# Chunk attention and a feed-forward layer on one core: scores and values as four 64x64 tiles from the tenth group on

## The chip, the cores and the metric

The kernel runs on one core of one Trainium2 chip. The metric is the device time of an execution in microseconds (us). Three runs of the kernel before took 304.3, 305.3 and 305.69 us; their median is 305.3 us.

## The reference

The inputs q, k and v are 8 batches x 8 heads x 576 positions x 64 in float32. Attention stays within chunks of 64 positions, so a batch has nine chunks:

```
scores = scale * q_c @ k_c^T            # 64 x 64 for each batch, head and chunk
scores = scores - max(scores)
attn   = exp(scores);  attn = attn / (sum(attn) + 1e-9)
out    = attn @ v_c                     # 64 x 64
x = out laid out as (8*576 tokens, 8*64 = 512)
h = x @ w_in                            # 512 -> 2048
y = maximum(0.01 h, h) @ w_out          # 2048 -> 512
```

The output is 4608 x 512 in float32.

## The kernel before, in words

The 4608 tokens go through attention in 36 groups (u = 0 to 35) of two chunks (128 tokens, all eight heads). The result of a group is written transposed into xT (features on partitions, tokens along the free axis), and the feed-forward layer takes xT in blocks of 128, 256 and 512 tokens (BLOCKS, L57). All is computed in float16 with float32 sums.

A group passes through these stages, each a function:

- The transposes of q and k. Groups 0 to 8 load token rows (load_qk, L71) and transpose them on TensorE (stage_t, L255) into the PSUM tiles qp and kp; DVE copies q to QZ and ACT copies k to KT. From group UD = 9 on, that is from batch 2 on, load_qk_batch (L89) brings a whole batch in blocks of 32 to the tiles q_d and k_d, and DVE transposes the blocks straight into QZ (stage_dq, L290, one call for each half s of the partitions) and KT (stage_dk, L298).
- Scores (stage_s, L306). Two heads sit on the 128 partitions of q and k, each with its 64 features. QZ holds each q block in a 128x128 frame whose other two quarters are zeros, so that one matmul gives 64 scores of two heads on 128 output partitions. Eight matmuls of 64 columns fill the PSUM tile Sp.
- Softmax: stage_m (L316, DVE: maximum and subtraction from PSUM), stage_x (L325, ACT: exp), stage_n (L329, DVE: sum, reciprocal, product into en).
- The transposes of en (stage_e, L342, four on TensorE into tpe) and their copy by DVE (stage_c, L349) to et.
- Values (stage_v, L355). VB holds v of one batch with a zero block beside each 64 columns; there are two such buffers. Eight matmuls of 64 columns fill xp. stage_a (L372, ACT) copies xp to xT.

The feed-forward layer is cut into chunks of work: mm1 (L161: matmuls from w_inT and xT into hT, then ACT's leaky ReLU into gT) and mm2 (L182: four matmuls from gT and w_outT into oP, after the last of four ACT's copy to osb and the store). fill(n) (L228) issues the next n chunks whose tokens are there.

The order on each engine is the order of the program text, written by hand. The first five groups and the start of others follow the list FRONT (L415), with dummy matmuls ("i"). The loop at L428 does the rest: in turn it come scores and softmax of group it-1, a fill of 2 chunks, the transposes of en of group it-2, the q and k transposes of group it, again 2 chunks, the values of group it-2, then 3 chunks. So each turn has 28 matmuls of the feed-forward layer of 512 columns, once the blocks are large. What is left of that layer follows the loop.

All loads go through POOL's queue in program order: first the list LOADS (L147: g for q and k of a group, v for a batch of v, Q and P for quarters of the weights, D2 for q and k of batch 2), then v of batch b+2 after the last values of batch b (L368), and q and k of batches 3 to 7 at turns given by L454. The stores go through SP's queue.

PSUM has eight banks: mm takes four, qp, kp, Sp and ox (shared by tpe and xp) one each.

Of the kernel before, what the change touches and what calls it, by code (L numbers as in the profile page):

```python
# [8 lines left out]
FP16 = mybir.dt.float16  # L9
FP32 = mybir.dt.float32  # L10
ALU = mybir.AluOpType
AFT = mybir.ActivationFunctionType
AXL = mybir.AxisListType
# [3 lines left out]
def kernel(  # L17
# [6 lines left out]
    moe_w_out: bass.AP,  # L24
    out: bass.AP,
):

    nc = tc.nc

    B, H, S, D = q.shape
# [3 lines left out]
    CH = 64  # L45
    NCH = S // CH
# [3 lines left out]
    NQZ = 3  # L50
    NVB = 2
    NIN = 9
    UD = 9
    G = 2 * CH
# [4 lines left out]
    sbp = ctx.enter_context(tc.tile_pool(name="k_sb", bufs=1))  # L59
    psp = ctx.enter_context(tc.tile_pool(name="k_ps", bufs=1, space=bass.MemoryType.PSUM))  # L60
# [2 lines left out]

    VB = [sbp.tile([128, H // 2, NCH, 128], FP16, name=f"VB{i}") for i in range(NVB)]
    QZ = [sbp.tile([128, 4, 2, 2, CH], FP16, name=f"QZ{i}") for i in range(NQZ)]
    w_inT = sbp.tile([128, NT, d_ff], FP16, name="w_inT")
    w_outT = sbp.tile([128, NFC, d_model], FP16, name="w_outT")
    xT = sbp.tile([128, NT, n_tok], FP16, name="xT")
# [40 lines left out]
    def load_v(b):  # L109
        for m in range(2):  # L110
            nc.gpsimd.dma_start(  # L111
                out=VB[b % NVB][m * CH:(m + 1) * CH, :, :, m * CH:(m + 1) * CH].rearrange("p h c d -> p (h c) d"),
                in_=v[b, m * H // 2:(m + 1) * H // 2].rearrange("h (c j) d -> j (h c) d", j=CH),
            )

    def load_w_in(f0, f1):
        for m in range(2):
            nc.gpsimd.dma_start(  # L118
                out=w_inT[m * CH:(m + 1) * CH, :, f0:f1],
                in_=moe_w_in[m * d_model // 2:(m + 1) * d_model // 2, f0:f1].rearrange("(t d) f -> d t f", d=D),  # L120
            )
# [14 lines left out]
    for eng, name, src in ((nc.sync, "q_f", q), (nc.scalar, "k_f", k)):  # L136
        t = sbp.tile([128, H, D], FP32, name=name)
# [7 lines left out]
    qk[0] = tuple(sbp.tile([128, H, D], FP16, name=n, tag=n, bufs=NIN) for n in ("q_in", "k_in"))  # L145

    LOADS = (  # L147
        "g1 v0 Q1 Q0 g2 Q2 Q3 g3 g4 P0 g5 P2 P3 P1 g6 v1 g7 g8 D2 "
    )
    LOADERS = {"g": load_qk, "v": load_v, "Q": load_w_in_quarter, "P": load_w_out_quarter, "D": load_qk_batch}  # L150
    ident = sbp.tile([128, 128], FP16, name="ident")
    for n, what in enumerate(LOADS.split()):
        LOADERS[what[0]](int(what[1:]))
        if n == 0:
# [6 lines left out]
    def mm1(j, a):  # L161
        tb, r0 = BLOCKS[j], START[j]
        nf = 512 // tb
        if j not in gT:
            tag, bufs, pad = ("gS", 6, 128) if tb == 128 else ("gT", 2, 512)
            gT[j] = sbp.tile([128, NFC, tb], FP16, name="gT", tag=tag, bufs=bufs, padded_shape=[128, NFC, pad])
        hT = psp.tile([128, nf, tb], FP32, name="hT", tag="mm", bufs=4)
        for i in range(nf):
            fc = nf * a + i
            for t in range(NT):  # L170
                nc.tensor.matmul(  # L171
                    out=hT[:, i, :],
                    lhsT=w_inT[:, t, fc * 128:(fc + 1) * 128],
                    rhs=xT[:, t, r0:r0 + tb],
                    start=(t == 0),
                    stop=(t == NT - 1),
                )
        nc.scalar.activation(  # L178
            out=gT[j][:, nf * a:nf * a + nf, :], in_=hT, func=AFT.Prelu, bias=0.0, scale=1.0, alpha=0.01
        )  # L180
# [45 lines left out]
    state = {"tokens": 0}  # L226
# [19 lines left out]
    KP: dict[int, bass.AP] = {}  # L246
    SP: dict[int, bass.AP] = {}
    KT: dict[int, bass.AP] = {}
    SH: dict[int, bass.AP] = {}
    E: dict[int, bass.AP] = {}  # L250
    TP: dict[int, bass.AP] = {}
# [2 lines left out]

    def stage_t(u):  # L255
        qt, kt = qk.pop(u)
        qp = psp.tile([128, 4, 2, CH], FP16, name="qp", tag="qp", bufs=1)
        kp = psp.tile([128, 4, 2, CH], FP16, name="kp", tag="kp", bufs=1)
        for i in range(4):
            nc.tensor.transpose(out=qp[:, i, :, :], in_=qt[:, 2 * i:2 * i + 2, :], identity=ident)  # L260
        for i in range(4):
            nc.tensor.transpose(out=kp[:, i, :, :], in_=kt[:, 2 * i:2 * i + 2, :], identity=ident)  # L262
        QP[u], KP[u] = qp, kp

    def stage_q(u, halves=(0, 1)):
        for s in halves:
            part = slice(s * CH, (s + 1) * CH)
            nc.vector.tensor_copy(out=QZ[u % NQZ][part, :, :, s, :], in_=QP[u][part])

    def stage_w(u, halves=(0, 1)):  # L270
        for s in halves:
            part = slice(s * CH, (s + 1) * CH)
            nc.scalar.activation(
                out=QZ[u % NQZ][part, :, :, s, :], in_=QP[u][part], func=AFT.Copy, bias=0.0, scale=1.0
            )
# [9 lines left out]
    def cuts(u):  # L285
        r0, r1 = u * G, (u + 1) * G
        cut = min(-(-r0 // S) * S, r1) if r0 % S else r1
        return [(a // S, a % S, (a - r0) // CH, (z - a) // CH) for a, z in ((r0, cut), (cut, r1)) if a < z]

    def stage_dq(u, s):  # L290
        qz = QZ[u % NQZ]
        for b, at, e0, n in cuts(u):
            nc.vector.transpose(  # L293
                out=qz[s * CH:(s + 1) * CH, :, e0:e0 + n, s, :],
                in_=qkd[b][0][s * CH:(s + 1) * CH, :, at:at + n * CH].rearrange("p h (e t) -> p h e t", e=n),
            )

    def stage_dk(u):  # L298
# [7 lines left out]
    def stage_s(u):  # L306
        qz, kt = QZ[u % NQZ], KT.pop(u)
        Sp = psp.tile([128, 8, CH], FP32, name="Sp", tag="Sp", bufs=1)
        for i in range(8):
            g, e, m = i // 4, i // 2 % 2, i % 2  # L310
            nc.tensor.matmul(  # L311
                out=Sp[:, i, :], lhsT=qz[:, 2 * m + g, e, :, :], rhs=kt[:, 2 * m + g, e, :], start=True, stop=True
            )
        SP[u] = Sp

    def stage_m(u):  # L316
        Sp = SP.pop(u)
        mx = sbp.tile([128, 8], FP32, name="mx", tag="mx", bufs=2)
        nc.vector.tensor_reduce(out=mx, in_=Sp, axis=AXL.X, op=ALU.max)  # L319
        SH[u] = sbp.tile([128, 8, CH], FP32, name="sh", tag="sh", bufs=2)  # L320
        nc.vector.tensor_tensor(  # L321
            out=SH[u], in0=Sp, in1=mx.unsqueeze(2).to_broadcast((128, 8, CH)), op=ALU.subtract
        )

    def stage_x(u):  # L325
        E[u] = sbp.tile([128, 8, CH], FP16, name="ex", tag="ex", bufs=2)
        nc.scalar.activation(out=E[u], in_=SH.pop(u), func=AFT.Exp, bias=0.0, scale=SCL)  # L327
# [21 lines left out]
    def stage_c(u):  # L349
        tpe = TP.pop(u)  # L350
        et = sbp.tile([128, 2, 2, 2, CH], FP16, name="et", tag="et", bufs=2)
        nc.vector.tensor_copy(out=et, in_=tpe)  # L352
        ET[u] = et

    def stage_v(u):  # L355
        et = ET.pop(u)
        xp = psp.tile([128, NT, 2, CH], FP32, name="xp", tag="ox", bufs=1)
        for e in range(2):
            b, c = divmod(2 * u + e, NCH)
            for t in range(NT):  # L360
                nc.tensor.matmul(  # L361
                    out=xp[:, t, e, :],
                    lhsT=VB[b % NVB][:, t, c, :],
                    rhs=et[:, t // 2, e, t % 2, :] if u < UD else et[:, t % 2, e, t // 2, :],
                    start=True,
                    stop=True,
                )
            if c == NCH - 1 and b + NVB < B:  # L368
                load_v(b + NVB)
        XP[u] = xp  # L370

    def stage_a(u):  # L372
        xp = XP.pop(u)
        nc.scalar.activation(out=xT[:, :, u * G:(u + 1) * G], in_=xp, func=AFT.Copy, bias=0.0, scale=1.0)  # L374
        state["tokens"] = (u + 1) * G
# [21 lines left out]
    def empty(i):  # L397
        i, m = divmod(i, 2)
        return VB[i][m * CH:(m + 1) * CH, :, :, (1 - m) * CH:(2 - m) * CH]

    def zero(i):
        nc.vector.memset(QZ[i] if i < NQZ else empty(i - NQZ), 0.0)

# [24 lines left out]
    for it in range(6, NU + 2):  # L428
        dve = UD <= it < NU
        if it <= NU:  # L430
            stage_s(it - 1)
            stage_m(it - 1)
        if dve:
            stage_dq(it, 0)
        fill(2)
        if it <= NU:
            stage_x(it - 1)
        stage_e(it - 2)
        stage_c(it - 2)
        if dve:  # L440
            stage_dq(it, 1)
            stage_dk(it)
        elif it < UD:
            stage_t(it)
            stage_q(it)
            stage_k(it)
        if it <= NU:
            stage_n(it - 1)
        fill(2)
        stage_v(it - 2)  # L450
        stage_a(it - 2)
        fill(3 if dve else 2)
        for b in range(3, B):
            if it == 9 * b // 2 - 4:  # L454
                load_qk_batch(b)
# [31 lines left out]
```

## Time and profile before

| what | value |
|---|---|
| median of three runs | 305.3 us (304.3 to 305.69) |
| span of the profiled execution, first to last instruction | 303.1 us |
| time of the profiled execution around its span | not given by the page; the median lies 2.2 us above the span |
| granted TensorE clock over the span | 1.000 |
| DVE: max (L319), subtraction (L321), sum (L332), product (L338) | 0.691, 0.691, 0.653, 0.692 us each |
| DVE's copy to et (L352) | 0.416 us each |
| q_d and k_d issues on POOL | 48 + 48, 0.820 and 0.815 us each |
| v issues on POOL | 16, 1.165 us each |
| from issue to landing: v, q_d, k_d (median) | 6.4, 4.0, 4.3 us |

How to read it: PE is TensorE's matmuls, PEld its weight loads, DVE VectorE, ACT ScalarE, POOL GpSimd. A group's row gives the line, the engine, the operation, output and input tiles, the shape and the count; behind the first bar the busy time in us and the mean length of one in ns; behind the second the idle time of the engine just before, and what ended it. "128*128" in a TensorE row is the part of the array in use. The chain of work that ended last is followed back from the last instruction, so its pieces are the time that sets the end.

### The profile page before, as it was taken

The page shows a single profiled execution, that of the slowest core. Times are in us where ns is not written, and L with a number is a line of the kernel's source. Part 1 is how long each engine was busy: PE and PEld are TensorE (multiplying, and loading weights), DVE is VectorE, ACT ScalarE, POOL GpSimd, SP SyncE. Part 2 cuts the span into 40 slices and gives each one's busy share as a digit, 9 for nine tenths or more (in the row PEclk, how much of TensorE's full clock was granted, in tenths as well). Part 3 has the DMA queues.
Part 4 walks back from the last instruction along what each step waited for, and adds up shares of the span by engine and source line. Part 5 has one row for each costly group of instructions (what it writes and reads, how often), then busy time and mean ns, then how long its engine had stood idle before and what let it go on. Part 6 is the DMA issues. An engine that isn't in the chain of part 4 may idle for free.

```text
span 303.1 us, 6057 instructions
## 1 busy us (share of the span) xinstructions
PE 290.7 (96%) x2504; PEld 180.5 (60%) x2504; DVE 193.6 (64%) x368; ACT 155.6 (51%) x268; POOL 119.6 (39%) x148
## 2 busy tenths in 40 slices
PE   5869999999999999999999999999999999999995
PEld 5768965676768685858555555554555554444444
DVE  3747776777888888878888888888888850000000
ACT  6336753564647373737377337723773377227511
POOL 8567747999108832970079329700000000000000
PEclk9999999999999999999999999999999999999999
DMA  9999999999919991999099929991100110011011
GB/s 135 157 188 164 184 169 174 166 150 141 121 70 56 124 127 38 126 109 107 35 86 96 114 83 124 76 106 69 37 0 37 69 37 0 35 69 38 0 69 70
DMA packets 177643, 28.44 MB, mean 94 GB/s; under 512 B 168784, under 2 KB 173136, under 8 KB 177616
## 3 DMA queue, kind: packets, MB, share of 16 engines
q0 software_dynamic: 170208, 18.10, 106.1%
q1 hardware_dynamic: 6368, 9.70, 9.0%
q10 hardware_dynamic: 1040, 0.26, 0.4%
q8 instruction: 19, 0.31, 0.4%
q14 instruction: 8, 0.07, 0.1%
HBM read 36.70 MB, written 9.44 MB: 152 GB/s over the span
## 4 chain that ended last, share of the span: by engine, by line
PE 83%; DMA 11%; POOL 4%; issue 1%; ACT 0%; POOLq 0%
PE oP L187 38%; PE hT L171 37%; DMA w_inT<-in_moe_w_in_dram 6%; DMA VB<-in_v_dram 5%; PE xp L361 2%; PE Sp L311 2%; PE tpe L346 2%; PE oP L206 1%; POOL VB L111 1%; POOL k_in L80 1%; POOL q_in L80 1%; POOL w_outT L130 1%; POOL w_inT L118 0%; PE qp L260 0%; PE kp L262 0%
## 5 line engine op out<-in xcount | busy, mean ns | idle before, releaser
L171 PE MATMUL hT<-xT,w_inT 128*128 128x256 f16 (+2 forms) x960 | 135.3, 294 | 2.2 <-DMA w_inT<-in_moe_w_in_dram 2.2
L187 PE MATMUL oP<-w_outT,gT 128*128 128x512 f16 x560 | 130.2, 379 | 0.1
L178 ACT ACTIVATE gT<-hT 128x512 f16<-128x512 f32 x144 | 85.7, 597 | 37.1 <-PE hT L171 36.9
L171 PEld LDWEIGHTS <-w_inT 128*128 128x128 f16 x960 | 80.8, 98 | 38.9 <-issue 2.4
L187 PEld LDWEIGHTS <-gT 128*128 128x128 f16 x560 | 51.8, 98 | 53.7 <-issue 0.3
L98 POOL DMA_DIRECT2D q_d<-in_q_dram x48 | 38.8, 820 | 57.0 <-DVE QZ L293 53.3
L196 ACT ACTIVATE osb<-oP 128x512 f32<-128x512 f32 x35 | 20.9, 597 | 70.9 <-PE oP L187 68.0
L319 DVE TENSOR_REDUCE mx<-Sp 128x8 f32<-128x512 f32 x36 | 24.9, 691 | 34.1 <-PE Sp L311 34.0
L293 DVE STREAM_TRANSPOSE QZ<-q_d 64x512 f16<-64x512 f16 (+1 forms) x60 | 38.2, 644 | 0.8
L98 POOL DMA_DIRECT2D k_d<-in_k_dram x48 | 38.6, 815 | 0.1
L374 ACT ACTIVATE xT<-xp 128x512 f16<-128x512 f32 x36 | 21.4, 593 | 17.4 <-PE xp L361 17.4
L327 ACT ACTIVATE ex<-sh 128x512 f16<-128x512 f32 x36 | 22.5, 625 | 10.5 <-DVE sh L321 10.2
L332 DVE TENSOR_REDUCE z<-ex 128x8 f32<-128x512 f16 x36 | 23.5, 653 | 3.5 <-ACT ex L327 3.4
L338 DVE TENSOR_TENSOR en<-ex,zi 128x512 f16<-128x512 f16 x36 | 24.9, 692 | 1.2
L321 DVE TENSOR_TENSOR sh<-Sp,mx 128x512 f32<-128x512 f32 x36 | 24.9, 691 | 1.2
L111 POOL DMA_DIRECT2D VB<-in_v_dram x16 | 18.5, 1165 | 6.1 <-PE xp L361 6.1
L301 DVE STREAM_TRANSPOSE KT<-k_d 128x512 f16<-128x512 f16 (+1 forms) x30 | 19.4, 654 | 0.8
L352 DVE COPY et<-tpe 128x512 f16<-128x512 f16 x36 | 15.0, 416 | 5.9 <-PE tpe L346 5.8
L361 PEld LDWEIGHTS <-VB 128*128 128x128 f16 x288 | 13.2, 98 | 6.7 <-issue 0.7
L311 PEld LDWEIGHTS <-QZ 128*128 128x128 f16 x288 | 13.1, 98 | 5.8
L346 PEld LDWEIGHTS <-en 128*128 128x128 f16 x144 | 10.8, 98 | 7.5 <-DVE en L338 1.2
L381 PE MATMUL idle<-ident 128*128 128x128 f16 x160 | 11.3, 233 | 3.8 <-POOL ident masks.py:199 3.8
(35 smaller groups left out, 136.8 us busy)
## 6 DMA issues: line engine op xcount, KB each, us to landing
out_dram<-osb SPq DMA_DIRECT2D x35, 256.0 KB, 2.0
VB<-in_v_dram POOLq DMA_DIRECT2D x16, 288.0 KB, 6.4
q_d<-in_q_dram POOLq DMA_DIRECT2D x48, 72.0 KB, 4.0
k_d<-in_k_dram POOLq DMA_DIRECT2D x48, 72.0 KB, 4.3
w_inT<-in_moe_w_in_dram POOLq DMA_DIRECT2D x8, 256.0 KB, 9.9
w_outT<-in_moe_w_out_dram POOLq DMA_DIRECT2D x4, 512.0 KB, 9.1
q_in<-in_q_dram POOLq DMA_DIRECT2D x7, 128.0 KB, 10.4
k_in<-in_k_dram POOLq DMA_DIRECT2D x7, 128.0 KB, 9.4
```

The costliest lines, as they stand in the source:

```text
L98: nc.gpsimd.dma_start(out=t[p0:p0 + 32, m, :, :, :].rearrange("p h b d -> p (h b) d"), in_=src[b, h0:h0 + 2, :, dh * 32:dh * 32 + 32].rear ...
L111: nc.gpsimd.dma_start(out=VB[b % NVB][m * CH:(m + 1) * CH, :, :, m * CH:(m + 1) * CH].rearrange("p h c d -> p (h c) d"), in_=v[b, m * H // ...
L171: nc.tensor.matmul(out=hT[:, i, :], lhsT=w_inT[:, t, fc * 128:(fc + 1) * 128], rhs=xT[:, t, r0:r0 + tb], start=(t == 0), stop=(t == NT - 1),)
L178: nc.scalar.activation(out=gT[j][:, nf * a:nf * a + nf, :], in_=hT, func=AFT.Prelu, bias=0.0, scale=1.0, alpha=0.01)
L187: nc.tensor.matmul(out=o, lhsT=gT[j][:, fc, ti * 128:(ti + 1) * 128], rhs=w_outT[:, fc, :], start=(fc == 0), stop=(fc == NFC - 1),)
L293: nc.vector.transpose(out=qz[s * CH:(s + 1) * CH, :, e0:e0 + n, s, :], in_=qkd[b][0][s * CH:(s + 1) * CH, :, at:at + n * CH].rearrange("p ...
L319: nc.vector.tensor_reduce(out=mx, in_=Sp, axis=AXL.X, op=ALU.max)
L321: nc.vector.tensor_tensor(out=SH[u], in0=Sp, in1=mx.unsqueeze(2).to_broadcast((128, 8, CH)), op=ALU.subtract)
L327: nc.scalar.activation(out=E[u], in_=SH.pop(u), func=AFT.Exp, bias=0.0, scale=SCL)
L332: nc.vector.tensor_reduce(out=z, in_=ex, axis=AXL.X, op=ALU.add)
L338: nc.vector.tensor_tensor(out=E[u], in0=ex, in1=zi.unsqueeze(2).to_broadcast((128, 8, CH)), op=ALU.mult)
L374: nc.scalar.activation(out=xT[:, :, u * G:(u + 1) * G], in_=xp, func=AFT.Copy, bias=0.0, scale=1.0)
```

## The change

From group 9 on, each 128x128 weight block with two zero quarters is replaced by its two full quarters, as matmuls of 64x64 weights that address a quarter of the array each. A quarter's rows are the partitions of its operands (s for scores, the half with head s; for values the half with the positions of one head), its columns are the output partitions.

- stage_s4 takes the place of stage_s: 16 matmuls of 64 columns, ordered i, s, e, so that each next matmul is on another quarter. Their output Sp2 has two banks, one for each s. stage_m4 does what stage_m did from two banks.
- stage_v4 takes the place of stage_v: 16 matmuls ordered e, g, s, m, into two xp tiles, one in the bank of Sp and one in that of ox. stage_a4 copies them with two ACT instructions of 256 elements in place of one of 512.
- q needs no zeros, so stage_dq is one DVE transpose of 128 partitions into QT, in place of two of 64 into QZ.
- v needs no zeros: VN has two buffers, a new one, and one in the space of VB[0]. load_vn brings a batch in four DMAs in place of two. v of batch 2 is loaded at the end of LOADS, ahead of D2; v of batch 3 after the last values of batch 0; the later ones, as before, after the last values of the batch two before.
- qp and kp become two halves of one PSUM tile of two banks ("two", one buffer), which Sp2 uses later on.
- The gS tiles have four buffers in place of six.

The diff without its blank lines:

```
+    VN = [
+        sbp.tile([128, H // 2, NCH, CH], FP16, name="VN0"),
+        VB[0].rearrange("p h c d -> p (h c d)")[:, 0:H // 2 * NCH * CH].rearrange("p (h c d) -> p h c d", h=H // 2, c=NCH),
+    ]
...
+    def load_vn(b):
+        for s in range(2):
+            for m in range(2):
+                h0 = 4 * m + 2 * s
+                nc.gpsimd.dma_start(
+                    out=VN[b % NVB][s * CH:(s + 1) * CH, 2 * m:2 * m + 2].rearrange("p h c d -> p (h c) d"),
+                    in_=v[b, h0:h0 + 2].rearrange("h (c j) d -> j (h c) d", j=CH),
+                )
...
-        "g1 v0 Q1 Q0 g2 Q2 Q3 g3 g4 P0 g5 P2 P3 P1 g6 v1 g7 g8 D2 "
+        "g1 v0 Q1 Q0 g2 Q2 Q3 g3 g4 P0 g5 P2 P3 P1 g6 v1 g7 g8 n2 D2 "
...
-            tag, bufs, pad = ("gS", 6, 128) if tb == 128 else ("gT", 2, 512)
+            tag, bufs, pad = ("gS", 4, 128) if tb == 128 else ("gT", 2, 512)
...
     def stage_t(u):
         qt, kt = qk.pop(u)
-        qp = psp.tile([128, 4, 2, CH], FP16, name="qp", tag="qp", bufs=1)
-        kp = psp.tile([128, 4, 2, CH], FP16, name="kp", tag="kp", bufs=1)
+        two = psp.tile([128, 2, 8, 2, CH], FP16, name="qkp", tag="two", bufs=1)
+        qp, kp = two[:, 0, 0:4], two[:, 1, 0:4]
...
-    def stage_dq(u, s):
-        qz = QZ[u % NQZ]
+    def stage_dq(u):
+        QT[u] = sbp.tile([128, 4, 2, CH], FP16, name="QT", tag="QT", bufs=2)
         for b, at, e0, n in cuts(u):
             nc.vector.transpose(
-                out=qz[s * CH:(s + 1) * CH, :, e0:e0 + n, s, :],
-                in_=qkd[b][0][s * CH:(s + 1) * CH, :, at:at + n * CH].rearrange("p h (e t) -> p h e t", e=n),
+                out=QT[u][:, :, e0:e0 + n, :],
+                in_=qkd[b][0][:, :, at:at + n * CH].rearrange("p h (e t) -> p h e t", e=n),
             )
...
+    def stage_s4(u):
+        qt, kt = QT.pop(u), KT.pop(u)
+        Sp = psp.tile([128, 2, 8, CH], FP32, name="Sp2", tag="two", bufs=1)
+        for i in range(4):
+            for s in range(2):
+                for e in range(2):
+                    d = slice(s * CH, (s + 1) * CH)
+                    nc.tensor.matmul(
+                        out=Sp[e * CH:(e + 1) * CH, s, i, :], lhsT=qt[d, i, e, :], rhs=kt[d, i, e, :],
+                        start=True, stop=True,
+                    )
+        SP[u] = Sp[:, :, 0:4, :]
+
+    def stage_m4(u):
+        Sp = SP.pop(u)
+        mx = sbp.tile([128, 2, 4], FP32, name="mx", tag="mx", bufs=2)
+        nc.vector.tensor_reduce(out=mx, in_=Sp, axis=AXL.X, op=ALU.max)
+        SH[u] = sbp.tile([128, 4, 2, CH], FP32, name="sh", tag="sh", bufs=2)
+        nc.vector.tensor_tensor(
+            out=SH[u].rearrange("p i s k -> p s i k"), in0=Sp, in1=mx.unsqueeze(3).to_broadcast((128, 2, 4, CH)),
+            op=ALU.subtract,
+        )
+        SH[u] = SH[u].rearrange("p i s k -> p (i s) k")
...
-        ET[u] = et
+        ET[u] = et if u < UD else et.rearrange("p a b e q -> p (a b) e q")
...
+            if c == NCH - 1 and b == 0:
+                load_vn(3)
+        XP[u] = xp
+
+    def stage_v4(u):
+        et = ET.pop(u)
+        xp = [psp.tile([128, 2, 2, CH], FP32, name="xp", tag=tag, bufs=1) for tag in ("Sp", "ox")]
+        for e in range(2):
+            b, c = divmod(2 * u + e, NCH)
+            for g in range(2):
+                for s in range(2):
+                    for m in range(2):
+                        j = slice(s * CH, (s + 1) * CH)
+                        nc.tensor.matmul(
+                            out=xp[s][m * CH:(m + 1) * CH, g, e, :],
+                            lhsT=VN[b % NVB][j, 2 * m + g, c, :],
+                            rhs=et[j, 2 * m + g, e, :],
+                            start=True,
+                            stop=True,
+                        )
             if c == NCH - 1 and b + NVB < B:
-                load_v(b + NVB)
+                load_vn(b + NVB)
         XP[u] = xp
+
+    def stage_a4(u):
+        for s, xp in enumerate(XP.pop(u)):
+            nc.scalar.activation(
+                out=xT[:, 2 * s:2 * s + 2, u * G:(u + 1) * G], in_=xp, func=AFT.Copy, bias=0.0, scale=1.0
+            )
+        state["tokens"] = (u + 1) * G
```

In the loop, group it-1 takes stage_s4 and stage_m4 when it is 9 or later, group it-2 takes stage_v4 and stage_a4 when it is 9 or later, and stage_dq is called once, where its first half stood.

More of the change, by code (lines that the diff above doesn't have):

```diff
@@ L147 @@
     LOADS = (
-        "g1 v0 Q1 Q0 g2 Q2 Q3 g3 g4 P0 g5 P2 P3 P1 g6 v1 g7 g8 D2 "
+        "g1 v0 Q1 Q0 g2 Q2 Q3 g3 g4 P0 g5 P2 P3 P1 g6 v1 g7 g8 n2 D2 "
     )
-    LOADERS = {"g": load_qk, "v": load_v, "Q": load_w_in_quarter, "P": load_w_out_quarter, "D": load_qk_batch}
+    LOADERS = {"g": load_qk, "v": load_v, "Q": load_w_in_quarter, "P": load_w_out_quarter, "D": load_qk_batch, "n": load_vn}
     ident = sbp.tile([128, 128], FP16, name="ident")
@@ L248 @@
     KT: dict[int, bass.AP] = {}
+    QT: dict[int, bass.AP] = {}
     SH: dict[int, bass.AP] = {}
@@ L430 @@
         if it <= NU:
-            stage_s(it - 1)
-            stage_m(it - 1)
+            if it - 1 < UD:
+                stage_s(it - 1)
+                stage_m(it - 1)
+            else:
+                stage_s4(it - 1)
+                stage_m4(it - 1)
         if dve:
-            stage_dq(it, 0)
+            stage_dq(it)
         fill(2)
@@ L440 @@
         if dve:
-            stage_dq(it, 1)
             stage_dk(it)
@@ L449 @@
         fill(2)
-        stage_v(it - 2)
-        stage_a(it - 2)
+        if it - 2 < UD:
+            stage_v(it - 2)
+            stage_a(it - 2)
+        else:
+            stage_v4(it - 2)
+            stage_a4(it - 2)
         fill(3 if dve else 2)
```

## The prediction

> **What bounds the kernel now.** I read the page's first part, then the chain of work that ended last, then that chain in order of time, then the groups kept apart by shape, and last the timelines of POOL and DVE around the tenth group.
>
> ```profile
> PE 290.7 (96%) x2504; PEld 180.5 (60%) x2504; DVE 193.6 (64%) x368; ACT 155.6 (51%) x268; POOL 119.6 (39%) x148
> PE 83%; DMA 11%; POOL 4%; issue 1%; ACT 0%; POOLq 0%
> ```
>
> The second line is the chain: TensorE holds it, and DMA only in the first 47 us (weights and v). From 47.0 us to 299.5 us the chain in order of time has only PE pieces without a gap. One turn of the loop in the middle of it (start us, us, what):
>
> ```profile
> 146.87 0.23 PE xp L361 x8
> 147.10 2.59 PE oP L187 x12
> 149.69 0.23 PE Sp L311 x8
> 149.93 0.86 PE oP L187 x4
> 150.79 0.86 PE hT L171 x4
> 151.65 0.22 PE tpe L346 x4
> 151.88 1.73 PE hT L171 x8
> 153.60 0.23 PE xp L361 x8
> ```
>
> A turn takes 153.60 - 146.87 = 6.73 us, and it is wholly matmuls: 28 of 512 columns at 1.73/8 = 0.216 us, the scores (Sp) 0.23, the values (xp) 0.23, the transposes of the weights of attention (tpe) 0.22. So what the change does to the end is what it does to the two pieces of 0.23 us, if nothing else becomes late. Eight matmuls of 64 columns in 0.23 us are 0.029 us each.
>
> ```profile
> L187 PE MATMUL oP<-w_outT,gT 128*128 128x512 f16 x560 | 130.2, 379 | 0.1
> L361 PE MATMUL xp<-et,VB 128*128 128x64 f16 x288 | 14.4, 193 | 0.5 <-DVE et L352 0.3 <-DMA VB<-in_v_dram 0.2
> L311 PE MATMUL Sp<-KT,QZ 128*128 128x64 f16 x288 | 14.3, 193 | 0.0
> L361 PEld LDWEIGHTS <-VB 128*128 128x128 f16 x288 | 13.2, 98 | 6.7 <-issue 0.7
> L311 PEld LDWEIGHTS <-QZ 128*128 128x128 f16 x288 | 13.1, 98 | 5.8
> L293 DVE STREAM_TRANSPOSE QZ<-q_d 64x512 f16<-64x512 f16 x48 | 33.6, 701 | 0.7
> L301 DVE STREAM_TRANSPOSE KT<-k_d 128x512 f16<-128x512 f16 x24 | 17.1, 711 | 0.8
> L374 ACT ACTIVATE xT<-xp 128x512 f16<-128x512 f32 x36 | 21.4, 593 | 17.4 <-PE xp L361 17.4
> L214 ACT ACTIVATE osb<-oP 128x256 f32<-128x256 f32 x2 | 0.8, 384 | 2.5 <-PE oP L206 2.5
> ```
>
> The reader is to see two things. A matmul lasts much longer than the distance to the next: 0.379 against 0.216 us at 512 columns, 0.193 against 0.029 at 64. The difference, 0.163 and 0.164 us, is its tail in the pipeline, hidden today because the next one follows in the same form. And a weight load lasts 0.098 us but costs nothing, since it begins while earlier matmuls run.
>
> **The change on TensorE.** Groups 9 to 35 are 27 groups with two stages each: 54 stages, which today cost 54 x 0.23 = 12.4 us. That is all that can be won. Each stage becomes 16 weight loads and 16 matmuls of 64x64 instead of 8 and 8 of 128x128, in an order that goes round the four tiles, and two borders appear: from full-array matmuls to quarter tiles and back. No row of this trace has a tile smaller than 128x128, so both prices are bounded.
>
> The 16 matmuls: from below, four tiles at once, so four rounds of 0.029 = 0.116 us (each tile still has to stream four times 64 columns). From above, one after another at today's distance, 16 x 0.029 = 0.464 us. I take 0.116, since the four use separate rows, columns and PSUM banks and the order changes tile with each matmul.
>
> The two borders: from below nothing, if the array takes the other form in mid-stream. From above, the tail of the matmul ahead is waited out and the first load after it is bare: 0.163 + 0.098 into the stage and 0.164 + 0.098 out of it, 0.523 us in all. I take the two tails without the loads, 0.327 us: a tail is what every matmul row here has, and nothing in the trace shows a matmul of another form running into one, while loads are seen to go ahead of the matmuls before them in every stage. Bare loads stay as the upper end.
>
> A stage is then 0.116 + 0.327 = 0.443 us against 0.23, that is +0.213, and 54 of them **+11.5 us**. A turn would go from 6.73 to 7.16 us.
>
> [...]
>
> **The rest of the change, at nothing, with its cover.** DVE: one transpose of q of 128x512 (0.711, as k's row shows) replaces two of 64x512 (0.701 each): 0.69 us less of a turn in which DVE works 5.7 of 6.73 us (0.691 + 0.691 + 2 x 0.701 + 0.416 + 0.711 + 0.653 + 0.276 + 0.203 + 0.692). Max and subtraction read as many elements from two banks. No PE piece waits for DVE after 47 us, so nothing is won; the cover only grows. ACT: two copies of 128x256 (0.384) replace one of 0.593, +0.175 a turn on an engine with 51% busy; the tokens become ready that much later, but after the last values at 253.5 us the chain still has 45 us of feed-forward matmuls, so the order runs far behind the tokens. Gone cover would cost 27 x 0.175 = 4.7 us. The shared PSUM tile "two" makes the q transposes of a group wait for the copy of the k before; that copy lies a turn back from 47 us on, and ahead of that DMA ends the waits. Scores wait for the subtraction of the group before, which ended 5 us earlier. The gS buffers go from six to four, and there are four blocks of that kind.
>
> POOL: v of batch 2 goes ahead of q and k of batch 2, in four DMAs. POOL's timeline before:
>
> ```profile
> start us, us, engine line op out<-in xcount [idle before <-releaser]
> 52.05 6.43 POOL L98 DMA_DIRECT2D k_d<-in_k_dram  x8
> 58.48 2.32 POOL L111 DMA_DIRECT2D VB<-in_v_dram  x2
> ```
>
> On DVE's timeline k of group 9 is taken here:
>
> ```profile
> 65.16 0.71 DVE L301 STREAM_TRANSPOSE KT<-k_d 128x512 f16<-128x512 f16 x1
> ```
>
> The last k issue begins near 57.7 us and lands about 4.3 us later (median of these DMAs), at 62.0; DVE takes k at 65.16 and the scores of group 9 start at 68.49, so k may be late by 68.49 - 0.71 - 62.0 = 5.8 us. The four new issues cost between 0.81 (a q_d issue, a quarter the rows of today's v issue) and 1.16 us each (a v issue, twice their rows): 3.2 to 4.6 us, inside the slack. If the queue is full there and the whole 8.7 us of issue and landing (2.3 + 6.4) is added, PE stands once for 8.7 - 5.8 = 2.9 us. I take 0 and keep 0 to +2.9. Later v loads keep their places or come a batch earlier.
>
> **Sum.** The page gives no time of the profiled execution but its span, 303.1 us; the median of the runs, 305.3, is 2.2 above, which I take as what lies around the span. 303.1 + 11.5 + 2.2 = **316.8 us**, 3.8% over the median.
>
> **Rivals.**
> 1. Four tiles at once and no price at the border: a stage of 0.116 us, 54 x (0.116 - 0.23) = -6.2, so 299.1 us, faster. For it: tiles have rows and banks of their own, and half of each weight block today is zeros. Against it: the tails of 0.16 us are real and something must end them. It decides as long as a border costs under (0.23 - 0.116)/2 = 0.057 us. [...]
> 2. The change doesn't do what it says: no border price, but the small matmuls go one after another at 0.029 us. 0.464 - 0.23 = +0.234, x 54 = +12.6, so 317.9 us. For it: 64 columns cost 0.029 us today whatever the weights are. Near the forecast in time, but the loss would lie within the stage and not at its borders. [...]
> 3. Borders with bare loads: 0.116 + 0.523 = 0.639, +0.409 x 54 = +22.1, so 327.4 us. [...]
> 4. Tails and one after another: 0.327 + 0.464 = 0.791, +30.3 us, 335.6.
> 5. A border that costs part of a tail, 0.03 to 0.10 us: 54 x (0.176 to 0.316 - 0.23) = -2.9 to +4.6, so 302.4 to 309.9 us.
>
> **Chances.** Forecast 0.32; rival 1 0.26 (0.21 faster, 0.05 within, if the rounds are somewhat slower than 0.029); rival 2 0.17; rival 3 0.10; rival 4 0.05; rival 5 0.10 (0.01 faster, 0.05 within, 0.04 slower). About 0.5% (1.5 us) is what a measurement of this kernel can tell from no change. Faster 0.22, within 0.10, slower 0.32 + 0.17 + 0.10 + 0.05 + 0.04 = 0.68. The range goes from rival 1 to just above rival 3, 299 to 328 us; rival 4 and the edges of 1 and 3 stay out. The likeliest case's own range is 314 to 320: a stage 0.05 us cheaper on the one side, the late k on the other.
>
> **What would show it.** Right: turns of about 7.16 us, with a stage of about 0.44 us from its first matmul's predecessor to its successor, small matmuls starting in quick succession and a gap of about 0.16 us at both borders. Rival 1: turns near 6.5 us and no gap. Rival 2: 16 starts at 0.029 us without border gaps. Rival 3: gaps of 0.26 us. A PE wait for KT or en near 68 us would show the late k. The prediction is wrong above all if TensorE changes form without a stop, or if PE starts to wait for DVE or ACT.

## The result

The changed kernel takes 312.5 us (median of four runs, 311.79 to 312.61) against 304.8 us for the kernel before (four runs, 303.66 to 305.69). The ratio is 1.0238, with a 95% interval of 1.0209 to 1.0268: slower by 2.4%. The profiled execution took 312.57 us with a span of 310.8 us, against a span of 303.1 us before: +7.7 us.

The profile after, first its engines and its chain:

```profile
PE 297.7 (96%) x2936; PEld 174.9 (56%) x2936; DVE 172.6 (56%) x338; ACT 157.2 (51%) x295; POOL 126.2 (41%) x160
PE 89%; DMA 6%; POOL 2%; DVE 1%; ACT 1%; issue 1%; ACTq 0%; POOLq 0%
```

TensorE still sets the end. The chain in order of time, a turn in its middle (start us, us, what):

```profile
150.32 0.25 PE xp L407 x16
150.57 2.70 PE oP L188 x12
153.27 0.25 PE Sp L325 x16
153.52 0.97 PE oP L188 x4
154.49 0.86 PE hT L172 x4
155.35 0.22 PE tpe L372 x4
155.57 1.73 PE hT L172 x8
157.30 0.25 PE xp L407 x16
```

A turn takes 157.30 - 150.32 = 6.98 us, 0.25 us more than the 6.73 before. The pieces of the values and the scores grew only from 0.23 to 0.25 us. The rest is in the full matmuls that follow them: 2.70 us for twelve in place of 2.59, 0.97 for four in place of 0.86. A piece of the chain goes from the modelled end of what ran before it to its own modelled end. So the stop ahead of a stage lies in the stage's own piece, and the stop behind it in the piece of the full matmuls that come next. The groups of the small matmuls and their loads:

```profile
L325 PE MATMUL Sp<-KT,QT 64*64 64x64 f16 x432 | 8.6, 198 | 0.0
L325 PEld LDWEIGHTS <-QT 64*64 64x64 f16 x432 | 5.6, 107 | 10.2 <-issue 10.2
```

The scores' matmuls are busy for 8.6 us in 27 groups, where the 14.3 us of before for 36 groups make 10.7 for 27, and still the kernel is slower: busy time does not hold the stops. They leave a mark in the second line: 10.2 us, 0.38 us a stage, in which the weight loads stood although nothing in the profile held them. That is more than the stop, since no load goes ahead there while the last full matmul runs: the first load of a stage starts 0.002 us before its own matmul. Before, it started 0.214 us before it, and the loads of the scores had 5.8 us of idle time over 36 groups. The starts of single instructions in the trace put numbers to it (medians; before 36 stages of each kind, after 27):

| from start to start, us | before | after |
|---|---|---|
| last full matmul to first of the stage (512 columns ahead) | 0.216 | 0.309 |
| first to last of the stage | 0.203 (8) | 0.126 (16) |
| last of the stage to next full matmul | 0.029 | 0.125 |
| that one to the one after it | 0.216 | 0.226 |

So a stage takes 0.309 - 0.216 + 0.126 + 0.125 + 0.010 = 0.354 us of TensorE, against 0.203 + 0.029 = 0.232 before. The difference, 0.122 us, times 54 is 6.6 us; followed through the trace, the changed kernel falls behind by 0.241 us a turn, 6.5 us in 27 turns, by nearly the same step in each. Of the other 1.2 us, it is 0.8 us behind at 62 us, ahead of the first small matmul, and 0.4 us come after the last matmul: from its start to the end of the span 4.19 us pass, in place of 3.83. The same holds for every kernel below: 4.18 to 4.20 us in those made from the changed kernel, 3.83 to 3.84 in those made from the one before. What takes it I did not follow up.

Inside a stage four starts lie 0.003 to 0.004 us apart, the first of the next four follows 0.053 us after the first, and the later rounds 0.032 us after the one before. A bare load is one that could not go ahead and starts just before its own matmul; the first four matmuls of a stage have bare loads and last 0.213 us, the others 0.193. So the stage is four rounds of 0.032 = 0.128 us, 0.020 for the bare loads of the first round, 0.093 ahead, 0.093 behind (0.125 - 0.032), 0.010 by which the fourth start of a round lies behind its first, and 0.010 for the bare load of the full matmul, together 0.354. All but the four rounds is the price of the two borders, 0.226 us, and the work itself is cheaper than before by 0.104.

### The profile page after: what moved, and what is told of

It reads as the page before. It is cut to its first block, busy times and chain, and to the rows that moved or that the text cites. A ratio compares the mean times of both kernels' runs of the same rounds, so it can differ in the third digit from the quotient of the medians.

```text
span 310.8 us, 6942 instructions
## 1 busy us (share of the span) xinstructions
PE 297.7 (96%) x2936; PEld 174.9 (56%) x2936; DVE 172.6 (56%) x338; ACT 157.2 (51%) x295; POOL 126.2 (41%) x160
## 4 chain that ended last, share of the span: by engine, by line
PE 89%; DMA 6%; POOL 2%; DVE 1%; ACT 1%; issue 1%; ACTq 0%; POOLq 0%
PE oP L188 40%; PE hT L172 39%; DMA w_inT<-in_moe_w_in_dram 3%; DMA k_in<-in_k_dram 3%; PE tpe L372 2%; PE xp L407 2%; PE Sp L325 2%; PE oP L207 1%; POOL VB L103 1%; POOL w_inT L119 1%; PE xp L387 1%; DVE QZ L270 1%; PE Sp L313 0%; PE qkp L264 0%; ACT KT L285 0%
## 5 line engine op out<-in xcount | busy, mean ns | idle before, releaser
L334 DVE TENSOR_REDUCE mx<-Sp 128x8 f32<-128x512 f32 x27 | 18.7, 691 | 54.4 <-PE Sp L325 54.4
L420 ACT ACTIVATE xT<-xp 128x256 f16<-128x256 f32 x54 | 17.7, 384 | 11.4 <-PE xp L407 11.4
L336 DVE TENSOR_TENSOR sh<-Sp,mx 128x512 f32<-128x512 f32 x27 | 18.7, 692 | 0.9
L295 DVE STREAM_TRANSPOSE QT<-q_d 128x512 f16<-128x512 f16 (+1 forms) x30 | 19.1, 644 | 0.0
L434 PE MATMUL idle<-ident 128*128 128x128 f16 x160 | 11.5, 235 | 3.8 <-POOL ident masks.py:199 3.8
L372 PE MATMUL tpe<-ident,en 128*128 128x128 f16 x144 | 14.0, 220 | 0.9 <-DVE en L364 0.7
L112 POOL DMA_DIRECT2D VN<-in_v_dram x12 | 10.2, 865 | 8.7 <-PE xp L407 6.2
L112 POOL DMA_DIRECT2D VB<-in_v_dram x12 | 10.2, 866 | 6.6 <-PE xp L407 6.1
```

Of the source, the lines that this page charges most:

```text
L112: nc.gpsimd.dma_start(out=VN[b % NVB][s * CH:(s + 1) * CH, 2 * m:2 * m + 2].rearrange("p h c d -> p (h c) d"), in_=v[b, h0:h0 + 2].rearran ...
L295: nc.vector.transpose(out=QT[u][:, :, e0:e0 + n, :], in_=qkd[b][0][:, :, at:at + n * CH].rearrange("p h (e t) -> p h e t", e=n),)
L372: nc.tensor.transpose(out=tpe[:, i, :], in_=en[:, 2 * i:2 * i + 2, :], identity=ident)
```

## The experiments

**Theory A**: the price belongs to the border, a fixed sum each time the array leaves its full form and comes back. **Theory B**: it belongs to the many small loads and matmuls. **Theories C and D** are about 0.8 us by which the changed kernel is behind at 62 us, ahead of the first small matmul.

### One small matmul by itself

In the kernel before, at two places in each of 27 turns, between two feed-forward chunks:

```
+    def small():
+        t = psp.tile([128, 4, CH], FP32, name="small", tag="qp", bufs=1)
+        nc.tensor.matmul(out=t[0:CH, 0, :], lhsT=ident[0:CH, 0:CH], rhs=ident[0:CH, 0:CH], start=True, stop=True)
...
-        fill(2)
+        fill_around(2, it)
```

fill_around(2, it) does fill(1), small(), fill(1) in turns 10 to 36, and fill(2) in the others.

> The kernel before with one extra matmul of 64x64 weights and 64 columns at two places in each of 27 turns, between feed-forward chunks (54 in all; its result is not used). Theory A (the price lies at the border, each time the array goes to quarter tiles and back, whatever the number of matmuls between): by the trace after, 0.093 us ahead of the first, 0.125 us from the last start to the next full matmul and 0.010 us on the one after, together +0.228 us each, 54 x 0.228 = +12.3 us. Theory B (the price belongs to the many small loads and matmuls, 0.122 us over 16 of them): 0.008 to 0.029 us each, +0.4 to +1.6 us.

Measured: 318.8 us against 305.2 us, ratio 1.0434 (1.0399 to 1.0469), +13.6 us. The chain of this kernel:

```profile
149.67 0.86 PE oP L187 x4
150.54 0.14 PE small L385
150.68 0.97 PE oP L187 x4
151.65 0.22 PE tpe L346 x4
151.87 0.86 PE oP L187 x4
152.74 0.14 PE small L385
152.88 0.97 PE oP L187 x4
```

One matmul of 64 columns has a piece of 0.14 us and makes that of the four full ones behind it 0.11 us longer, as in the changed kernel: 0.97 in place of 0.86. By single starts it adds 0.093 + 0.146 + 0.010 = 0.249 us, times 54 is 13.4 us. Theory B, at most 1.6 us, falls. Of the amount above theory A's 12.3 us, 1.1 us is the bare load of 0.020 to 0.021 us that I had left out of it, 54 times.

### Which change of form makes the border

The same with `lhsT=ident[0:CH, :]` (64 rows, 128 columns) and with `lhsT=ident[:, 0:CH]`, `rhs=ident[:, 0:CH]` (128 rows, 64 columns).

> As the extra matmul of 64x64, but with 64 rows and all 128 columns of the array (weights of 64 partitions x 128). Theory A1 (splitting the rows makes the border): +12 us as with 64x64. Theory A2 (splitting the columns makes it): no border, 54 x 0.029 = +1.6 us. Theory A3 (any change of form): +12 us here and with 128x64.

> As the extra matmul of 64x64, but with all 128 rows and 64 columns of the array. Theory A1 (rows make the border): 54 x 0.029 = +1.6 us, somewhat more if the shorter load is slower. Theory A2 (columns make it) or A3 (any change of form): about +12 us.

Measured: 318.1 us (ratio 1.0418, 1.0382 to 1.0453) and 318.3 us (1.0426, 1.0391 to 1.0461). The groups of the three kernels:

```profile
L385 PE MATMUL small<-ident 64*64 64x64 f16 x54 | 11.5, 213 | 0.0
```

```profile
L385 PE MATMUL small<-ident 64*128 64x64 f16 x54 | 10.8, 199 | 0.0
```

```profile
L385 PE MATMUL small<-ident 128*64 128x64 f16 x54 | 11.7, 217 | 0.0
```

Half the rows, half the columns or both: the border is the same, 0.093 to 0.095 us ahead. Behind, the next full matmul starts after 0.146 us for 64x64, 0.132 for 64x128 and 0.149 for 128x64. Only the bare load differs: the matmul lasts 0.213, 0.199 and 0.217 us, where one with a hidden load lasts 0.193, and less that difference the three are 0.125 to 0.126 us. Each of the three changes of form stops TensorE (A3). The table of the result rules out two other causes, the 64 columns and the change of PSUM bank: in the kernel before, matmuls of 64 columns in full form stand between those of 512, in a PSUM bank of their own, and start with no stop (0.216 us ahead, 0.029 behind).

### The order of the quarters

In both stages of the changed kernel, four matmuls in a row on one quarter (here the scores; the loops of the values go s, m, e, g):

```
-        for i in range(4):
-            for s in range(2):
-                for e in range(2):
+        for s in range(2):
+            for e in range(2):
+                for i in range(4):
```

> The changed kernel with its 16 matmuls of each stage in another order: four in a row on one quarter, then the next quarter. Theory A with concurrency only between neighbours in the order: starts on the same quarter are 0.032 us apart, so 16 x 0.032 = 0.51 us in place of 4 x 0.032, up to +0.38 us a stage, up to 54 x 0.38 = +21 us over the changed kernel, less what the ends of two quarters overlap (3 x 0.029 at most, 16 us then). Rival: TensorE finds free quarters whatever the order, +0 us.

Measured: 314.1 us, ratio to before 1.0284 (1.0245 to 1.0323), 1.5 us over the changed kernel. By single starts, first to last takes 0.156 us in place of 0.126: +0.030, times 54 is 1.6 us. Nearly the rival. The first four starts are 0.013 us apart and each lasts 0.213 us, the length of a matmul with a bare load.

Three groups have their two chunks in two batches, so the weights of their values come from two buffers, VN for the first chunk and VB for the second. The program has VN, VN, VB, VB on each quarter in turn. The first of these groups on the timeline:

```profile
108.28 0.27 PE L407 MATMUL xp<-et,VN 64*64 64x64 f16 x7
108.37 0.19 PE L407 MATMUL xp<-et,VB 64*64 64x64 f16 x1
108.38 0.19 PE L407 MATMUL xp<-et,VN 64*64 64x64 f16 x1
108.38 0.25 PE L407 MATMUL xp<-et,VB 64*64 64x64 f16 x7
```

Seven matmuls with VN start before the first with VB, in all three groups: TensorE does not start them in the order of the program.

### Eight on one quarter

> The kernel before with eight extra matmuls of 64x64 at each of the 54 places, all on the same quarter of the array (results unused). If a quarter takes its matmuls one after another, at 0.029 to 0.032 us: seven more than the kernel with one, 54 x 7 x 0.03 = +11.5 us over its 318.8, about 330 us. If the starts 0.013 us apart, seen where four in a row go to one quarter, are the pace of a single quarter: 54 x 7 x 0.013 = +4.9 us, about 323.7 us.

Measured: 330.7 us, ratio 1.0867 (1.082 to 1.0915): the first of the two cases, +11.9 us over the kernel with one. After the first, which has a bare load, the starts are 0.032 us apart (0.052 from the first to the second), and only the first of the eight lasts 0.213 us. So one quarter takes its matmuls one after another, and the 0.032 us for four in the changed kernel is four quarters at work at once. It also explains the run before it: there the first four that started each had a bare load, so they were on four quarters, though the program has four on one quarter first. TensorE had taken matmuls of free quarters ahead of earlier ones. That the order is not kept is shown by the names VN and VB; which quarter each is on the trace does not name, so that part is worked out from lengths.

### Values and scores side by side

```
-        if it - 2 < UD:
-            stage_v(it - 2)
-            stage_a(it - 2)
-        else:
-            stage_v4(it - 2)
-            stage_a4(it - 2)
-        fill(3 if dve else 2)
+        if it - 2 < UD:
+            stage_v(it - 2)
+            stage_a(it - 2)
+            fill(3 if dve else 2)
+        else:
+            fill(3 if dve else 2)
+            stage_v4(it - 2)
+            stage_a4(it - 2)
```

> The changed kernel with the last three feed-forward chunks of a turn put ahead of the values instead of behind them, so that the values of group it-2 and the scores of group it follow each other and the array takes quarter tiles once a turn, not twice. Nothing else differs. Theory A (price at the border): a visit with 32 small matmuls costs 8 rounds x 0.032 + 0.226 = 0.482 us in place of two of 0.354, -0.226 us a turn, 26 turns: -5.9 us against the changed kernel, about 306.6 us. Theory B (price with the number of small matmuls): no difference, 312.5 us.

Measured: 306.8 us, ratio to before 1.0081 (1.005 to 1.0111), against 1.0238 for the changed kernel. Its chain:

```profile
150.19 0.25 PE xp L407 x16
150.44 0.13 PE Sp L325 x16
150.56 0.97 PE oP L188 x4
151.53 0.86 PE hT L172 x4
152.39 0.22 PE tpe L372 x4
152.62 4.32 PE hT L172 x20
156.93 0.25 PE xp L407 x16
```

The scores that follow the values cost 0.13 us, four rounds of 0.032 and nothing else, and the turn is 156.93 - 150.19 = 6.74 us, that of the kernel before. The small matmuls, their number and all else are as in the changed kernel; only half the borders are gone, and with them 5.7 us. This is theory A, forecast to 0.2 us.

### The shared PSUM tile

```
-        two = psp.tile([128, 2, 8, 2, CH], FP16, name="qkp", tag="two", bufs=1)
-        qp, kp = two[:, 0, 0:4], two[:, 1, 0:4]
+        qp = psp.tile([128, 8, 2, CH], FP16, name="qp", tag="qp", bufs=1)[:, 0:4]
+        kp = psp.tile([128, 8, 2, CH], FP16, name="kp", tag="kp", bufs=1)[:, 0:4]
...
-        Sp = psp.tile([128, 2, 8, CH], FP32, name="Sp2", tag="two", bufs=1)
+        Sp = [psp.tile([128, 8, CH], FP32, name="Sp2", tag=tag, bufs=1) for tag in ("qp", "kp")]
```

> The changed kernel with q and k transposed into two PSUM tiles again (one bank each, as before the change); the scores of a group go into two tiles of one bank, and DVE takes maximum and subtraction in two instructions of 256 elements each. Theory C (the 0.8 us by which the changed kernel is behind at 62 us comes from the shared tile: the next q transposes wait for the copy of k, and the copies of q and k no longer overlap): -0.8 us against the changed kernel, 311.7 us, and the second q transposes near 8.0 us instead of 9.0. Rival D (it comes from the earlier v load in POOL's queue): no difference. DVE's extra 0.28 us a turn should cost nothing.

> Both edits together: values and scores side by side, and separate PSUM tiles for q and k. Theories A and C: -5.9 - 0.8 = 305.8 us, about the time of the kernel before. If A holds and C does not: 306.6 us.

Measured: 312.3 us (1.0261, 1.0223 to 1.0298) and, with the stages side by side, 306.2 us (1.0047, 1.0018 to 1.0075). The wait is real: the second q transposes start at 9.03 us in the changed kernel, after 0.83 us in which TensorE stood for ACT's copy of k, and at 8.24 us with two tiles, with no wait. But the times differ by 0.3 and 0.6 us with overlapping intervals, so the gain is not shown. The start of the scores near 62 us says why. It is 61.56 us in the profile of before, 62.35 in the changed kernel and 62.02 with two tiles; in the four kernels with extra matmuls, whose program up to there is that of before, it is 62.55, 61.76, 62.30 and 60.85 us. The part up to there varies by more than the 0.8 us in question, so neither C nor D is settled, and the 0.8 us need no cause in the change.

### Two groups in a visit

The changed kernel with values of two groups and scores of two groups together in every second turn:

```
-    BLOCKS = [128] * 4 + [256] * 6 + [512] * 5
+    BLOCKS = [128] * 4 + [256] * 10 + [512] * 3
...
+    def visit(it):
+        if it == NU + 1:
+            vs, ss = (NU - 2, NU - 1), ()
+        else:
+            vs = {10: (), 12: (9,)}.get(it, (it - 4, it - 3))
+            ss = (it, it + 1) if it < NU else ()
+        if vs:
+            stage_v4(vs)
+        if ss:
+            stage_s4(ss)
+        if vs:
+            stage_a4(vs)
```

The rest of the edit puts the q and k transposes of a group a turn ahead and gives et three buffers.

> The changed kernel with one visit to quarter tiles every second turn: the values of two groups and then the scores of two groups, 64 small matmuls in a row. The values come two turns later, so two 512-token blocks of the feed-forward layer become four of 256 to keep it fed (about +0.3 us by today's 1.75 against 1.73 us for the same columns). Theory A (0.226 us for each visit, 0.032 us for each four matmuls): a full visit is 16 x 0.032 + 0.226 = 0.738 us against 4 x 0.232 = 0.928 us for the same work in full tiles. 11 full visits and five smaller ones come to -2.0 us against the kernel before, with the blocks -1.7 us: about 303.2 us, the first of these versions to be faster than the kernel before, by 0.6%. Theory B (price with the number of small matmuls, as in the changed kernel): 312 us, which the kernel with both stages side by side has already spoken against. If the turn becomes bound by DVE or ACT instead: PE waits appear and the time is above 305 us.

Measured: 305.9 us against 305.3, ratio 1.003 (1.0007 to 1.0052). It is 6.6 us faster than the changed kernel and not faster than the one before. Where a visit runs undisturbed it takes 0.747 us by single starts, where 0.738 was forecast:

```profile
223.32 0.38 PE xp L409 x32
223.69 0.27 PE Sp L326 x32
...
236.60 0.38 PE xp L409 x32
```

Two turns take 13.28 us, against 2 x 6.73 = 13.46. But one new wait came in, on the timeline:

```profile
90.07 0.38 PE L172 MATMUL hT<-xT,w_inT 128*128 128x256 f16 x2 [0.73 <-ACT xT L423]
```

With values two turns later, the order had run out of older tokens at group 9, and the next block needed what ACT was just copying: 0.73 us. Four visits also took 0.08 to 0.10 us longer than the others, for a reason that the trace does not show and that I did not follow up. From the scores near 62 us to the start of the last matmul the trace is 0.5 us shorter than that of the kernel before, about the 2.0 us less the wait, the four visits (0.4 together) and the blocks (0.3 by the estimate above). The 0.5 us are taken back outside: the scores near 62 us start 0.4 us later, and after the last matmul come the 0.35 us more that all kernels made from the changed one have.

## Why the prediction was right, and what it mis-sized

- **The bound and the place of the cost** held. TensorE had no idle time to hide the cost in, and what the change did to the end is what it did to two pieces of each turn: 6.5 of 7.7 us. The forecast was slower by 3.8%, 316.8 us; it is 2.4%, 312.5 us, inside the whole range, but below the 314 to 320 that I gave the likeliest case. The sum of what was measured is 303.1 + 6.5 for the stages + 0.8 ahead of them + 0.4 after the last matmul + 1.8 around the span (312.57 - 310.8; I had 2.2) = 312.6. I had nothing for the 0.8 and the 0.4.
- **The 16 matmuls**, taken as four rounds of 0.029 = 0.116 us: measured four rounds of 0.032. Four quarters do work at once; rivals 2 and 4 (one after another) are out, and 0.032 us for one quarter alone shows that it is concurrency and not shorter matmuls. I had given each quarter a PSUM bank of its own; two quarters share each of the two banks, and their starts are 0.003 to 0.004 us apart all the same.
- **The two borders** are the term that was mis-sized: 0.327 us for two whole tails of 0.163 was my estimate, and no run shows it; measured was 0.093 on either side. A tail is not the same as the stop. The tail is what the modelled length of a matmul has beyond the distance to the next (0.379 - 0.216), and only 0.093 of these 0.163 us passed before the matmul of the other form started. The stop is the same behind 512 columns (0.309 - 0.216) as behind 256 (0.203 - 0.110, in the kernel with one small matmul), so between these two it does not grow with the matmul ahead.
- **The bare loads**, left out with the reason that loads go ahead of matmuls: they do not go ahead across a border. In the trace after, the first load of a stage starts 0.002 us before its matmul. But they cost 0.020 and 0.010 us, not the 0.098 of their length, since a matmul starts some 0.002 to 0.004 us behind its load. So rival 3 (+22 us) was right that the loads are bare, at six times their price (0.196 against 0.030).
- Together a stage cost +0.122 us, where I had +0.213: 6.6 in place of 11.5 us. **Rival 5**, a border of part of a tail, was nearest in kind: its upper end, 0.10 us for each border, is close to the 0.093 measured; its time, up to 309.9 us, fell short by the loads, the slower rounds and what lies outside the stages. It is 2.6 us from the 312.5 measured, and the forecast is 4.3: that the forecast's range held is owed to its width. Rival 1 was wrong only in the border: at 0.113 us each with loads, it is twice the 0.057 below which that rival would have decided.
- A change of form costs a stop and a change of quarter does not: 0.093 to 0.095 us ahead of the matmul in each of three forms, and 0.003 to 0.004 us between starts on different quarters. Whether TensorE is empty at the stop, as I had taken it with a whole tail waited out, the runs do not show: the small matmul starts 0.309 us after a full one whose modelled length is 0.379.
- **The cover** held. DVE's one transpose of q takes 0.701 us, ACT's two copies 0.384 each, and no PE piece of the changed kernel waits for either past 62 us. For the shared PSUM tile I had said that ahead of 47 us only DMA ends the waits; that was wrong, by the 0.83 us that TensorE stood for the copy of k at 9 us, though no gain from taking it away is shown. k came late as the upper case supposed, but not by as much:

```profile
67.66 0.71 DVE L303 STREAM_TRANSPOSE KT<-k_d 128x512 f16<-128x512 f16 x1 [2.49 <-DMA k_d<-in_k_dram]
```

DVE stood 2.49 us for k, which landed 5.7 us after the 62.0 that I had reckoned for the kernel before, not 8.7. It was ready at 68.37, 0.84 us ahead of the scores at 69.21. The 0 that I took was right, by less than a microsecond.

## What to carry to other kernels

Count the borders, not the matmuls: leaving the full form of the array and coming back cost 0.21 to 0.24 us here with its bare loads, whether 1, 8, 16, 32 or 64 small matmuls lay between, while 16 small matmuls cost 0.13 us against 0.23 for the eight that they replace. By these figures a visit to quarter tiles pays only if it takes more than twice the work of one of these stages (0.226 / 0.104 = 2.2): with two stages in a visit a turn took 6.74 us against 6.73 before, with four two turns took 13.28 against 13.46. So stages that use them belong side by side. And the stop between two forms was in no busy time (8.6 us for the scores against 10.7 before, in a slower kernel): look for pieces of the chain that are longer than the same matmuls elsewhere (here those behind the border, 0.97 against 0.86 us), and for loads that no longer start ahead (here 0.002 us before their matmul, against 0.214).

## What the runs showed of the hardware beyond that

- The stop is the same, 0.093 to 0.095 us, for half the rows, half the columns and a quarter of the array.
- A quarter takes one matmul of 64 columns in 0.032 us, four quarters take four in the same time, and one full matmul of 64 columns takes 0.029 us.
- TensorE does not keep the order of matmuls between quarters: with four in a row on one quarter, 16 took 0.156 us from first to last start, where one quarter at 0.032 us would need 0.10 for its four before the next began, 0.4 us in all, and seven matmuls with weights from VN started before the first from VB, where the program has VN, VN, VB, VB.
